# Loading a weight in place and early, moving a normalisation to ScalarE, and giving an early output its own banks

## The chip, the cores and the metric

The kernel runs on one core of a Trainium2 chip. The metric is the device time of one execution, in microseconds (us). The kernel before takes 285.63 us in the median of its first three runs (285.40 to 285.96). A program on one core has no second die to compare with, so its runs are called fast unless they lie more than 1.5% above the fastest of the same kernel.

## The reference, cut to what matters

The inputs are 2048 rows of 640 columns in bfloat16. The result is the sum of a residual, a state-space layer (A) and a gated MLP with a spatial product (B).

```python
xn = layernorm(x)
# A: a complex diagonal recurrence over the 2048 rows
Bu   = xn @ B_bar.T                       # B_bar = ((Lam_bar-1)/Lam) * B
h[t] = Lam_bar * h[t-1] + Bu[t]
yA   = 2 * real(h @ C.T) + xn * Dskip
# B: a gated MLP with a 2048 x 2048 product over the rows
z    = gelu(xn @ w_in)                    # 2048 x 1728
z1, z2 = z[:, :864], layernorm(z[:, 864:])
g    = w_sp @ z2 + b_sp[:, None]          # "spatial"
yB   = (z1 * g) @ w_out
out  = x + yA + yB
```

## The kernel before

The kernel records every operation with the memory that it reads and writes. A list scheduler with a cost model of its own then deals the operations to the engines' queues. In the timelines below an operation that is ready still waits for those that stand ahead of it in its engine's queue (the eviction "u2" of set 4 was ready near 162.4 us and ran at 166.1). And any edit can deal the queues anew.

TensorE runs these stages: z2 tiles, the "bu" products (41.8 to 86.8 us), z1 tiles (to 116), then eight "product sets" j = 0..7 of seven products each. A set multiplies one eighth of `w_sp` with z2 by a seven-product (Strassen-like) scheme and takes 10.2 us; S1 to S4 and T1 to T4 are the combinations (sums) of blocks of `w_sp` and of z2 that these products take, made by VectorE. After sets 5 and 6 come two "early outputs" each; the other twelve outputs end the kernel. One output is 20 products of states with C ("oh") and 14 products of gated rows with `w_out` ("og").

The parts that the change and the argument touch, with cuts marked `...`:

```python
# memory: r2 first holds the tables and scratch of the scan, later the transposed gate tiles gT.
# The raw C tiles are staged in the SAME bytes as gT:
q2 = r2.again()
wo_m = q2.sub(7 * 1280)
gT_m = [q2.sub(1792) for _ in range(8)]
cr_m = Mem(gT_m[0].lo, 8 * 1792)
craw_m = [cr_m.sub(1280) for _ in range(10)]
...
def c_scaled():                     # C' = kappa * C, complex; 10 tiles of 128 x 640
    for q in range(5):
        ...                         # DMA transposes: craw[2q] <- C_re, craw[2q+1] <- C_im
    for q in range(5):
        for c, (x, y, op) in ...:
            act(... activation(o, y, Identity, scale=k2) ...)          # "cy": ScalarE
            dve(... scalar_tensor_tensor(o, x, k1, o, mult, op) ...)   # "cp": VectorE
...
def spatial(j, banks):              # one product set, PSUM banks X, Y, Z
    prod(X, "A11", "B11"); ev(p1, X)          # ev: eviction of the bank by ScalarE
    prod(Y, "S1", "T1");   ev(p5, Y)
    prod(X, "S2", "T2");   ev(u2, X)          # the "third eviction"
    prod(Z, "A12", "B21"); dve(c11 = Z + p1)
    prod(X, "S3", "T3");   ev(u3, X) ...      # needs bank X free: waits for u2
    prod(Y, "S4", "B22");  dve(c12 = Y + u2)
    prod(X, "A22", "T4");  ev(c21, X)
    ...                                       # gate: 4 tiles in a ring, then gT by DMA transpose
...
for j in range(8):
    ...
    spatial(j, (0, 1, 2) if j % 2 == 0 else (3, 4, 5))
    ...
    if j >= 5 and j < 7:
        next_out(2, [6])                      # both early outputs in banks 6 and 7
next_out(12, [6, 0, 2, 4])
```

"fix" below means the 70 operations that add the scan's state to the states of each row block: ScalarE scales (P and Q), VectorE adds. "Horner" and "scan" are VectorE's recurrence over the rows.

## Time and profile before

| | before |
|---|---|
| time, median | 285.63 us |
| TensorE busy | 270.0 of 282.6 us |
| TensorE waits after start-up | 0.98 + 2.88 + 0.92 + 0.92 us |
| granted clock | 0.993: half speed for 3.41 us inside the run |

TensorE is busy nearly all the time and its order of work is the same in both kernels, so only its waits and its clock can change. These are two lines of the page of the kernel before: busy time by engine, and the granted TensorE clock in tenths of full speed, in 40 slices of the span.

```profile
...
PE 270.0 (96%) x1584; PEld 159.7 (57%) x1584; DVE 228.7 (81%) x556; ACT 158.4 (56%) x278; POOL 26.1 (9%) x53
...
PEclk9999999999999999999999979999999999999999
...
```

The view of waits, kernel before, TensorE alone from 100 to 225 us (engine, line waited for, releaser: us in total, times, longest us):

```profile
...
PE ps L923 <- ACT arena L936: 2.9, 1, 2.9
PE ps L1005 <- DVE arena L1022: 1.8, 2, 0.9
PE ps L923 <- ACT arena L602: 1.0, 1, 1.0
```

L923 is the product of a set and L936 its ScalarE eviction; L1005 is the first product of an output and L1022 VectorE's addition that empties its banks; L602 is the last z1 eviction. The largest wait is the 2.9 us inside set 4. The timeline of ScalarE in the kernel before, around that wait (start us, length us, engine, line, operation, count, and the idle time before it):

```profile
...
159.54 0.62 ACT L936 ACTIVATE arena<-ps,arena 128x432 f32<-128x432 f32 x1 [0.36 <-PE ps L923]
160.06 1.53 ACT L842 ACTIVATE arena<-arena 128x640 bf16<-128x640 bf16 x2
161.50 0.50 ACT L934 COPY arena<-ps 128x432 f32<-128x432 f32 x1
161.90 0.83 ACT L842 ACTIVATE arena<-arena 128x640 bf16<-128x640 bf16 x1
162.63 2.55 ACT L718 ACTIVATE arena<-arena 128x512 bf16<-128x512 bf16 x4
165.08 0.62 ACT L709 ACTIVATE arena<-arena 128x512 bf16<-128x512 bf16 x1
165.60 1.11 ACT L936 ACTIVATE arena<-ps,arena 128x432 bf16<-128x432 f32 x2
...
```

L842 are C scalings ("cy"), L718 and L709 fixes, L936 and L934 evictions. From 159.54 on ScalarE never rests. The last line holds c21 of set 3 and then u2 of set 4, the eviction on which the bank X depends. Its product had ended near 162.4, and it ran at 166.1. Ahead of it stood C scalings, four fix scalings, h7 and c21.

The second early output of each pair also waits. The timeline of TensorE, kernel before, has these lines for the state products of the first and the second output:

```profile
...
182.75 2.88 PE L1005 MATMUL ps<-arena 128*128 128x320 bf16 x20
...
188.45 2.89 PE L1005 MATMUL ps<-arena 128*128 128x320 bf16 x20 [0.92 <-DVE arena L1022]
...
```

The second could not start before VectorE had emptied banks 6 and 7 of the first. From start to start it is 5.70 us (188.45 less 182.75), of which 0.92 us is idle.

Lastly, busy time of each engine in three stretches, kernel before (stretch, its length, busy us with instruction counts, then PEclk, DMA share and GB/s):

```profile
...
core 0: us, PE busy (x) PEld busy (x) DVE busy (x) ACT busy (x) POOL busy (x), PEclk, DMA share, GB/s
40.00:60.00 20.00, 20.00 (x92) 8.73 (x91) 14.66 (x39) 18.53 (x37) 4.33 (x6) 1.00 0.55 72
60.00:80.00 20.00, 20.00 (x91) 8.52 (x89) 20.00 (x42) 11.84 (x20) 0.00 (x0) 1.00 0.00 1
...
167.00:171.00 4.00, 4.00 (x16) 1.85 (x15) 3.42 (x8) 2.74 (x6) 0.00 (x0) 0.68 0.79 94
...
```

In the last stretch the mean clock is 0.68. The trace's clock record says half speed for 3.41 us, from 166.17 to 169.58. TensorE resumed only at 166.77, so the first 0.6 us of the half speed fell into the wait. The same view, for the 3.41 us before the half speed and for the half speed itself:

```profile
...
162.76:166.17 3.41, 1.13 (x7) 0.39 (x4) 3.41 (x10) 3.41 (x7) 0.00 (x0) 1.00 1.16 270
166.17:169.58 3.41, 2.81 (x8) 1.20 (x9) 3.41 (x9) 2.38 (x5) 0.00 (x0) 0.50 1.06 136
...
```

TensorE was idle for 2.28 of the 3.41 us (3.41 less 1.13) just before its clock halved.

### The profile page before, as it was taken

Reading aid. Unit: us, or ns where it says so; the run is one execution under the profiler, and the core shown is the slowest. Engines: PE = TensorE matmul, PEld = TensorE weight load, DVE = VectorE, ACT = ScalarE, POOL = GpSimd, SP = SyncE. Lnnn points to the kernel's source line nnn. Section 1 sums busy time; section 2 is a strip of 40 time slices with the busy share of each in tenths; the row PEclk is TensorE's granted clock in tenths of the full one; section 3 lists DMA queues with packets and bytes.
Section 4 is the critical chain, followed back from the end, with each engine's and each line's share of the span. In section 5 each row is a group of like instructions: output and inputs, shape, how many; then the busy total and the mean of one; then the engine's idle time right before and its main releaser. Section 6 shows DMA issues by size and latency. Waiting matters only on the chain.

```text
span 282.6 us, 4366 instructions
## 1 busy us (share of the span) xinstructions
PE 270.0 (96%) x1584; PEld 159.7 (57%) x1584; DVE 228.7 (81%) x556; ACT 158.4 (56%) x278; POOL 26.1 (9%) x53
## 2 busy tenths in 40 slices
PE   7799999999999999899999959989989999999995
PEld 2455554444446777555555525555555577777773
DVE  4899845899999999899999998999999616354442
ACT  3799999985447554323323889999999300000000
POOL 4355732300000000000000000000000000000000
PEclk9999999999999999999999979999999999999999
DMA  7998999200000333696599898929965244422211
GB/s 205 277 223 141 224 131 153 26 3 0 0 0 32 127 125 125 205 143 130 119 153 180 147 200 200 239 63 183 195 167 118 80 58 110 126 74 67 72 46 46
DMA packets 81186, 34.73 MB, mean 123 GB/s; under 512 B 68526, under 2 KB 81166, under 8 KB 81166
## 3 DMA queue, kind: packets, MB, share of 16 engines
q1 hardware_dynamic: 81022, 34.39, 56.3%
q8 instruction: 12, 0.20, 0.3%
q10 hardware_dynamic: 144, 0.08, 0.1%
q14 instruction: 8, 0.07, 0.1%
HBM read 12.29 MB, written 6.18 MB: 65 GB/s over the span
## 4 chain that ended last, share of the span: by engine, by line
PE 91%; DVE 3%; ACT 3%; DMA 1%; POOL 1%; issue 0%; SPq 0%; DVEq 0%
PE ps L923 28%; PE ps L559 19%; PE ps L617 16%; PE ps L1005 16%; PE ps L1013 11%; DMA arena<-in_A_x_dram 1%; PE ps L532 1%; ACT arena L718 1%; ACT arena L842 1%; DVE arena L505 1%; DVE arena L518 1%; DVE arena L1022 1%; DVE arena L506 1%; POOL arena L513 0%; ACT arena L936 0%
## 5 line engine op out<-in xcount | busy, mean ns | idle before, releaser
L923 PE MATMUL ps<-arena 128*128 128x432 bf16 x448 | 83.8, 350 | 3.9 <-ACT arena L936 2.9
L923 PEld LDWEIGHTS ps<-arena 128*128 128x128 bf16 x448 | 44.1, 99 | 43.1 <-ACT arena L936 3.3
L559 PE MATMUL ps<-arena 128*128 128x432 bf16 x320 | 60.4, 346 | 0.0
L559 PEld LDWEIGHTS ps<-arena 128*128 128x128 bf16 x320 | 38.2, 121 | 18.0
L1005 PE MATMUL ps<-arena 128*128 128x320 bf16 x320 | 46.1, 299 | 1.8 <-DVE arena L1022 1.8
L617 PE MATMUL ps<-arena 128*128 128x512 bf16 x200 | 45.2, 386 | 0.0
L718 ACT ACTIVATE arena<-arena 128x512 bf16<-128x512 bf16 x70 | 44.4, 719 | 0.0
L1005 PEld LDWEIGHTS ps<-arena 128*128 128x128 bf16 x320 | 31.1, 98 | 14.9 <-DVE arena L1022 2.5
L936 ACT ACTIVATE arena<-ps,arena 128x432 f32<-128x432 f32 (+1 forms) x32 | 19.7, 618 | 29.0 <-PE ps L923 29.0
L617 PEld LDWEIGHTS ps<-arena 128*128 128x128 bf16 x200 | 19.2, 96 | 25.8
L1013 PE MATMUL ps<-arena 128*128 128x320 bf16 (+1 forms) x224 | 33.1, 299 | 0.0
L1022 DVE TENSOR_TENSOR arena<-ps,arena 128x640 bf16<-128x640 f32 x15 | 12.3, 822 | 22.3 <-PE ps L1013 22.3
L624 ACT CAST arena<-ps 128x512 bf16<-128x512 f32 x40 | 21.3, 593 | 13.2 <-PE ps L617 13.2
L721 DVE TENSOR_TENSOR arena<-arena 128x512 bf16<-128x512 bf16 x70 | 26.7, 415 | 1.0 <-ACT arena L718 1.0
L1013 PEld LDWEIGHTS ps<-arena 128*128 128x128 bf16 (+1 forms) x224 | 21.9, 98 | 8.5
L648 DVE SCALAR_TENSOR_TENSOR arena<-arena 128x512 f32<-128x512 bf16 x35 | 25.5, 745 | 0.0
L880 DVE TENSOR_TENSOR arena<-arena 128x1024 bf16<-128x1024 bf16 x32 | 21.6, 684 | 1.7 <-PE ps L923 1.7
L602 ACT ACTIVATE arena<-ps 128x864 bf16<-128x864 f32 x16 | 14.2, 890 | 13.5 <-PE ps L559 12.4
L670 DVE TENSOR_TENSOR arena<-arena 128x512 f32<-128x512 f32 (+2 forms) x40 | 21.4, 553 | 0.0
L653 DVE SCALAR_TENSOR_TENSOR arena<-arena 128x256 bf16<-128x256 bf16 (+1 forms) x35 | 16.6, 479 | 0.0
L650 DVE SCALAR_TENSOR_TENSOR arena<-arena 128x256 bf16<-128x256 bf16 (+1 forms) x35 | 16.5, 477 | 0.0
L573 ACT ACTIVATE arena<-arena 128x864 bf16<-128x864 bf16 x16 | 14.9, 937 | 0.0
(88 smaller groups left out, 220.2 us busy)
## 6 DMA issues: line engine op xcount, KB each, us to landing
arena<-in_A_x_dram SPq DMA_DIRECT2D x32, 160.0 KB, 2.8
z_scratch<-arena SPq DMA_DIRECT2D x16, 216.0 KB, 1.9
arena<-z_scratch SPq DMA_DIRECT2D x8, 432.0 KB, 3.9
out_dram<-arena SPq DMA_DIRECT2D x15, 160.0 KB, 1.8
arena<-in_B_w_in_dram SPq DMA_DIRECT2D x10, 216.0 KB, 3.3
arena<-in_B_w_out_dram SPq DMA_DIRECT2D x1, 960.0 KB, 5.8
arena<-in_B_w_sp_dram SPq DMA_TRANSPOSE x32, 4.2
arena<-arena SPq DMA_TRANSPOSE x20, 3.3
```

The costliest lines, as they stand in the source:

```text
L559: r = e.matmul(ps[:, b + h, 0:FG], lhs(k), winv[:, k, hcol * FH + h * FG:hcol * FH + (h + 1) * FG], start=(k == 0), stop=(k == ND - 1))
L617: r = e.matmul(ps[:, b + ri, :], btv[:, ri, k, q * 128:(q + 1) * 128], rhs[k], start=(k == 0), stop=(k == ND - 1))
L624: act(lambda e, ri=ri: e.copy(o[:, ri, :, half, :], ps[:, b + ri, :].rearrange("p (m j) -> p j m", j=4)), [bank(b + ri)], [l_iv(q, jg * 4 ...
L648: dve(lambda e: e.scalar_tensor_tensor(tv, prev, lr, cur, op0=ALU.mult, op1=ALU.add), pr + [l_iv(q, j)] + cr, [t.iv()], cd(512) + PTR, nm ...
L670: tt = lambda o, a, b, op: (lambda e: e.tensor_tensor(o, a, b, op))
L718: act(lambda e, pv=pv, hv=hv, lo=lo, sc=sc: e.activation(pv, hv[:, lo:lo + 2, 1:257], ACT.Identity, scale=sc), [h.iv(), Civ(cn)], [m.iv()] ...
L721: dve(lambda e, m=m, lq=lq: e.tensor_tensor(lq, lq, m.ap(512), ALU.add), li + [m.iv()], li, cd(512, 2), "fix%s%d%d" % (nm, q, j))
L880: dve(lambda e: e.tensor_tensor(o.ap(1024), x.ap(1024), y.ap(1024), op), [x.iv(), y.iv()], [o.iv()], cd(1024, 2), "%s_%d" % (name, j))
L923: r = e.matmul(ps[:, bk, 0:FG], lv_[:, k, :], rv[k], start=(first and k == 0), stop=(k == 7), skip_group_check=True)
L936: act(lambda e: e.activation(o, pb(bk), ACT.Identity, bias=bias), [bank(bk)] + bi, [dst], ca(FG, psum=True, ptr=1), name)
L1005: r = e.matmul(ps[:, b + n, 0:320], hv[:, o:o + 128], cpv[:, ri, q, n * 320:(n + 1) * 320], start=(q == 0 and ri == 0), stop=False, skip_g ...
L1013: r = e.matmul(ps[:, b + n, 0:320], gv[0:kk, k, :], wov[0:kk, k, n * 320:(n + 1) * 320], start=False, stop=(k == 6), skip_group_check=True)
```

## The change

The change has three parts. C is loaded directly to its final place as soon as the B weights there are dead (about 87 us), and is scaled in place with small temporaries in the dead z1 buffers. The normalisation of z2 row tiles 8 to 15 goes from VectorE to ScalarE. And the first of two early outputs uses banks that the next product set doesn't need yet, so that the second doesn't wait for its banks.

```diff
-        cr_m = Mem(gT_m[0].lo, 8 * 1792)
-        craw_m = [cr_m.sub(1280) for _ in range(10)]
+        cy_m = [Mem(z1o_m[0].lo, 3 * 1728).again()]
+        cy_m = [cy_m[0].sub(1280) for _ in range(4)]
...
+        ACT_Z2 = (8, 12)
...
+            if t0 in ACT_Z2:
+                dve(... v(7) = -mean * rstd ...)
             for i in range(t0, t1):
                 z = z2v[:, i, :]
+                if t0 in ACT_Z2:
+                    act(lambda e, i=i, z=z: e.activation(z, z, ACT.Identity, bias=st2v[:, 7, i:i + 1],
+                                                         scale=st2v[:, 6, i:i + 1]), ...)
+                    continue
                 dve(... (z - mean) * rstd ...)
...
-                    dma(... craw[2q], craw[2q+1] <- C_re, C_im ..., transpose=True)
+                    dma(... cpv[:, c, q, :] <- C_re, C_im ..., transpose=True)
...
-                    act(o = k2 * y);  dve(o = o +/- k1 * x)        # raw tiles to cpv
+                act(ta = k2 * im); act(tb = k2 * re)               # temporaries, two pairs
+                dve(re = k1 * re + ta); dve(im = tb - k1 * im)     # in place in cpv
...
-                next_out(2, [6])
+                next_out(2, [1 if j % 2 else 4, 6])
```

More of the change, by code (lines that the diff above doesn't have):

```diff
@@ L587, in z2_norm @@
                  0.33 + 0.165 * (t1 - t0), "z2r" + n)
+            if t0 in ACT_Z2:
+                dve(lambda e: e.scalar_tensor_tensor(v(7), v(2), -1.0, v(6), op0=ALU.mult, op1=ALU.mult),
+                    [vi(2), vi(6)], [vi(7)], 0.08, "z2b" + n)
             for i in range(t0, t1):
                 z = z2v[:, i, :]
+                if t0 in ACT_Z2:
+                    act(lambda e, i=i, z=z: e.activation(z, z, ACT.Identity, bias=st2v[:, 7, i:i + 1],
+                                                         scale=st2v[:, 6, i:i + 1]),
+                        [z2iv(i), s2iv(6, i, i + 1), s2iv(7, i, i + 1)], [z2iv(i)], ca(FH, ptr=2), "z2n%d" % i)
+                    continue
                 dve(lambda e, i=i, z=z: e.tensor_scalar(z, z, st2v[:, 2, i:i + 1], st2v[:, 6, i:i + 1],
@@ L831, in c_scaled @@
             for q in range(5):
-                raw = craw_m[2 * q:2 * q + 2]
-                for m, src, nm in ((raw[0], A_C_re, "r"), (raw[1], A_C_im, "i")):
-                    dma("sp", m.ap(D).rearrange("p (o n) -> p o n", o=1), src[:, q * 128:(q + 1) * 128], [], [m.iv()],
-                        D * 256, "C%s%d" % (nm, q), transpose=True)
+                for c, (src, nm) in enumerate(((A_C_re, "r"), (A_C_im, "i"))):
+                    dma("sp", cpv[:, c, q, :].rearrange("p (o n) -> p o n", o=1), src[:, q * 128:(q + 1) * 128], [],
+                        [cp_m.iv((c * 5 + q) * 1280, 1280)], D * 256, "C%s%d" % (nm, q), transpose=True)
@@ L836, in c_scaled @@
             for q in range(5):
-                re, im = craw_m[2 * q:2 * q + 2]
                 k1, k2 = C("k")[:, q:q + 1], C("k")[:, 5 + q:6 + q]
-                for c, (x, y, op) in enumerate(((re, im, ALU.add), (im, re, ALU.subtract))):
-                    o = cpv[:, c, q, :]
-                    oi = cp_m.iv((c * 5 + q) * 1280, 1280)
-                    act(lambda e, y=y, o=o, k2=k2: e.activation(o, y.ap(D), ACT.Identity, scale=k2),
-                        [y.iv(), Civ("k")], [oi], ca(D, ptr=1), "cy%d%d" % (q, c))
-                    dve(lambda e, o=o, x=x, k1=k1, op=op: e.scalar_tensor_tensor(
-                            o, x.ap(D), k1, o, op0=ALU.mult, op1=op, reverse1=(op == ALU.subtract)),
-                        [x.iv(), oi, Civ("k")], [oi], cd(D) + PTR, "cp%d%d" % (q, c))
+                re, im = cpv[:, 0, q, :], cpv[:, 1, q, :]
@@ new lines, in c_scaled @@
+                rei, imi = cp_m.iv(q * 1280, 1280), cp_m.iv((5 + q) * 1280, 1280)
+                ta, tb = cy_m[q % 2 * 2], cy_m[q % 2 * 2 + 1]
+                act(lambda e, o=ta, im=im, k2=k2: e.activation(o.ap(D), im, ACT.Identity, scale=k2),
+                    [imi, Civ("k")], [ta.iv()], ca(D, ptr=1), "cy%d0" % q)
+                act(lambda e, o=tb, re=re, k2=k2: e.activation(o.ap(D), re, ACT.Identity, scale=k2),
+                    [rei, Civ("k")], [tb.iv()], ca(D, ptr=1), "cy%d1" % q)
@@ L850, in t_comb @@
+                dve(lambda e, re=re, k1=k1, t=ta: e.scalar_tensor_tensor(re, re, k1, t.ap(D), op0=ALU.mult, op1=ALU.add),
+                    [rei, ta.iv(), Civ("k")], [rei], cd(D) + PTR, "cp%d0" % q)
+                dve(lambda e, im=im, k1=k1, t=tb: e.scalar_tensor_tensor(
+                        im, im, k1, t.ap(D), op0=ALU.mult, op1=ALU.subtract, reverse1=True),
+                    [imi, tb.iv(), Civ("k")], [imi], cd(D) + PTR, "cp%d1" % q)
         def t_comb(n):
```

## The prediction

> **What bounds it.** TensorE: busy 270.0 of 282.6 us (the page's first part), 91% of the chain of waits. Its order is the same in both kernels, so only its waits can go. The waits view shows: 0.98 us at 116.0 before the first product set, 2.88 us at 163.9 inside product set 4 (both on a ScalarE eviction), 0.93 + 0.86 us at 187.5 and 208.1, where the second early output waits for VectorE to empty the first's banks. The 2.88 us gap is followed by 8 matmuls 0.36 us apart instead of 0.18; the trace has the clock at half for 3.41 us from there, about 1.7 us lost. The Trainium skill ("TensorE: Matmul & The Clock Gate", Part 1) puts such a drop after an idle window of about 3.4 us; here 2.88 was enough and 0.9 to 1.0 us was not.
>
> **Cause of the big wait** (timeline). ScalarE runs without a pause from 159.5 to 167: seven C scalings (0.72 us apart), four "fix" scalings and h7 stand before the eviction that frees the bank. That one was ready at 162.4 and ran at 166.1. VectorE is full from 57 to 183, apart from about 1.4 us at 118.7, where the weight combination S4 of set 1 waits for a matmul to free its buffer.
>
> **What changes.**
> - C scaling: in the new order none of ScalarE's ten stands before that eviction, and VectorE's ten (0.80 us apart) stand among and after set 4's additions. Loads move to the z1 stage (DMA share 0.31 there), 1.25 us of queue time each: z1 stores may slip by 1 to 2 us, no TensorE wait expected.
> - z2 rows 8-15: VectorE loses 8 x 0.415 = 3.3 us, ScalarE gains 8 x about 1.0 (estimate: 0.72 for 512 columns, plus 352 x 0.83 ns), at 61-76 between evictions that take 0.96 of each 2.25 us: fits. I expect little from it: VectorE did that work while waiting for the sine tables (ready 54.5), and the T combinations that then filled the wait now come later. By a running sum of durations VectorE reaches S4 of set 1 near 117 to 119, waits there for the same matmul (120.1), and has 2.7 us of Horner/scan work behind that wait that stood ahead of it before.
> - Early outputs: both 0.9 us waits vanish, with 0.17 us of slower restart each: 2.1 us.
>
> **On the critical path.** Removed: 2.88 + 1.7 + 2.1 = 6.7 us. Returned: in the new order VectorE has, after set 4's fourth product at 163.7, about 15 us of work up to the last fix of row block 0, ending near 179; TensorE finishes set 5 at 178.3. The first early output should wait about 0.9 us, and slack at evictions of sets 4 and 5 is 0.2 to 0.4 us, so perhaps 0.4 more. Net about -5.4.
>
> **Time**: 280.2 us, 8 in 10 between 278.6 and 283.0. Faster by over 2%: 0.42, within 2%: 0.54, slower: 0.04.
>
> **To look for.** Right: no wait over 1.5 us inside sets 4-5; clock full from 20 us to the end; no wait at the second early outputs; a new wait of 0.5 to 2 us ahead of the first early output, on VectorE's fix or C addition; the wait at 116 unchanged; ScalarE near full at 60-80.
>
> **What would make it wrong.** A wait of 2 us or more inside set 4 or 5 again, halving the clock (283 and above); C transposes delaying z1 stores past three buffers; or VectorE gaining from the z2 move, so that the new wait vanishes (279).

The "running sum" in it works as follows: take each engine's new queue, give every operation the duration it has in the trace before, and carry the time forward, waiting where an operation needs another engine's result. The trace before gives 0.80 ns for each column (822 ns for 640 columns, 719 for 512, both with one per-partition operand), which leads to the same 1.0 us.

## The result, and the profile after

The changed kernel takes 279.17 us in the median (279.08 to 279.33, 4 runs), against 285.51 us (285.35 to 285.96, 4 runs) for the kernel before. The ratio is 0.9776, with a 95% interval from 0.9759 to 0.9793. Ratios here are the mean time of one kernel's fast runs over that of the other's fast runs of the same rounds, so they are not quite the ratio of the medians quoted.

The same lines of the page, kernel after:

```profile
...
PE 267.9 (97%) x1584; PEld 159.3 (57%) x1584; DVE 226.3 (82%) x550; ACT 166.7 (60%) x286; POOL 26.0 (9%) x53
...
PEclk9999999999999999999999999999999999999999
...
```

The clock is full from the second slice to the end, and TensorE's busy time is smaller by 2.1 us although it does the same matmuls (1.5 us of it in the product sets, where the half clock lay: 83.8 to 82.3 us). The waits of TensorE in the same window, kernel after:

```profile
...
PE ps L934 <- ACT arena L611: 1.0, 1, 1.0
PE ps L1016 <- DVE arena L730: 0.7, 1, 0.7
```

The wait in set 4 and both waits of the second early outputs are gone; the wait at the first set is unchanged. One wait is new: 0.7 us ahead of the first early output (L1016), on VectorE's last fix (L730). The timeline of ScalarE, kernel after, around u2 of set 4:

```profile
...
160.94 0.61 ACT L947 ACTIVATE arena<-ps,arena 128x432 bf16<-128x432 f32 x1
...
161.84 0.74 ACT L727 ACTIVATE arena<-arena 128x512 bf16<-128x512 bf16 x1
162.46 0.63 ACT L718 ACTIVATE arena<-arena 128x512 bf16<-128x512 bf16 x1
162.98 0.62 ACT L947 ACTIVATE arena<-ps,arena 128x432 f32<-128x432 f32 x1
164.12 0.83 ACT L849 ACTIVATE arena<-arena 128x640 bf16<-128x640 bf16 x1 [0.51 <-DVE arena L835]
...
```

Lines are numbered anew here: L947 and L945 are evictions, L727 fixes and L718 h7. The eviction u2 of set 4 is the line at 162.98. From 160.3 on only two fixes, c21 of set 3, the eviction p5 and h7 stand ahead of it; the first C scaling (L849) comes at 164.12. The timeline of TensorE, kernel after, at the first two outputs:

```profile
...
179.45 2.89 PE L1016 MATMUL ps<-arena 128*128 128x320 bf16 x20 [0.70 <-DVE arena L730]
...
184.08 2.88 PE L1016 MATMUL ps<-arena 128*128 128x320 bf16 x20
...
```

The second output (184.08) follows without an idle note, 4.63 us after the first: 1.07 us sooner than before. The three stretches, kernel after:

```profile
...
40.00:60.00 20.00, 20.00 (x93) 8.73 (x91) 11.29 (x35) 18.64 (x36) 4.14 (x6) 1.00 0.55 83
60.00:80.00 20.00, 20.00 (x91) 8.50 (x90) 17.95 (x37) 19.34 (x28) 0.00 (x0) 1.00 0.00 1
...
167.00:171.00 4.00, 4.00 (x24) 2.14 (x23) 4.00 (x7) 4.00 (x7) 0.00 (x0) 1.00 1.03 113
...
```

From 60 to 80 us ScalarE went from 11.84 to 19.34 us busy. VectorE is less busy by 5.4 us from 40 to 80 us: 3.3 us of that is the work moved away, and the rest is in the main waiting. The view of waits, kernel after, all engines, 40 to 225 us, has the T combinations (L870) waiting for ScalarE's normalised tiles (L595):

```profile
...
DVE arena L870 <- ACT arena L595: 2.0, 2, 1.7
...
```

### The profile page after: what moved, and what is told of

Read it like the earlier page. It is cut to its first block, busy times and chain, and to the rows that moved or that the text cites. A ratio compares the mean times of both kernels' runs of the same rounds, so it can differ in the third digit from the quotient of the medians.

```text
span 277.1 us, 4376 instructions
## 1 busy us (share of the span) xinstructions
PE 267.9 (97%) x1584; PEld 159.3 (57%) x1584; DVE 226.3 (82%) x550; ACT 166.7 (60%) x286; POOL 26.0 (9%) x53
## 4 chain that ended last, share of the span: by engine, by line
PE 88%; DVE 8%; DMA 1%; issue 1%; POOL 1%; ACT 0%; SPq 0%; DVEq 0%
PE ps L934 24%; PE ps L560 20%; PE ps L626 16%; PE ps L1016 16%; PE ps L1024 11%; DVE arena L854 1%; DVE arena L856 1%; DMA arena<-in_A_x_dram 1%; DVE arena L730 1%; PE ps L533 1%; DVE arena L506 1%; DVE arena L519 1%; DVE arena L891 1%; DVE arena L954 1%; DVE arena L507 1%
## 5 line engine op out<-in xcount | busy, mean ns | idle before, releaser
L934 PE MATMUL ps<-arena 128*128 128x432 bf16 x448 | 82.3, 346 | 1.0 <-ACT arena L611 1.0
L560 PE MATMUL ps<-arena 128*128 128x432 bf16 x320 | 60.4, 346 | 0.0
L1016 PE MATMUL ps<-arena 128*128 128x320 bf16 x320 | 46.1, 299 | 0.7 <-DVE arena L730 0.7
L727 ACT ACTIVATE arena<-arena 128x512 bf16<-128x512 bf16 x70 | 45.0, 713 | 1.0 <-DVE arena L730 0.9
L1016 PEld LDWEIGHTS ps<-arena 128*128 128x128 bf16 x320 | 31.2, 98 | 13.5 <-DVE arena L730 1.1
L947 ACT ACTIVATE arena<-ps,arena 128x432 f32<-128x432 f32 (+1 forms) x32 | 19.8, 617 | 29.1 <-PE ps L934 29.0
L730 DVE TENSOR_TENSOR arena<-arena 128x512 bf16<-128x512 bf16 x70 | 26.4, 418 | 1.3 <-ACT arena L727 1.1
L611 ACT ACTIVATE arena<-ps 128x864 bf16<-128x864 f32 x16 | 14.2, 890 | 13.5 <-PE ps L560 12.5
L679 DVE TENSOR_TENSOR arena<-arena 128x512 f32<-128x512 f32 (+2 forms) x40 | 21.2, 547 | 0.0
```

Source lines behind the costliest of these rows:

```text
L560: r = e.matmul(ps[:, b + h, 0:FG], lhs(k), winv[:, k, hcol * FH + h * FG:hcol * FH + (h + 1) * FG], start=(k == 0), stop=(k == ND - 1))
L679: tt = lambda o, a, b, op: (lambda e: e.tensor_tensor(o, a, b, op))
L727: act(lambda e, pv=pv, hv=hv, lo=lo, sc=sc: e.activation(pv, hv[:, lo:lo + 2, 1:257], ACT.Identity, scale=sc), [h.iv(), Civ(cn)], [m.iv()] ...
L730: dve(lambda e, m=m, lq=lq: e.tensor_tensor(lq, lq, m.ap(512), ALU.add), li + [m.iv()], li, cd(512, 2), "fix%s%d%d" % (nm, q, j))
L934: r = e.matmul(ps[:, bk, 0:FG], lv_[:, k, :], rv[k], start=(first and k == 0), stop=(k == 7), skip_group_check=True)
L947: act(lambda e: e.activation(o, pb(bk), ACT.Identity, bias=bias), [bank(bk)] + bi, [dst], ca(FG, psum=True, ptr=1), name)
```

## The experiments

All kernels gave correct results.

### The C part alone

Edit: the kernel after with `ACT_Z2 = ()` and `next_out(2, [6])`.

> The C part alone on the kernel before (early load, in-place scaling; no z2 move, no new banks). Theory (the 2.88 us wait in product set 4 came from where the C scaling stood, and its clock drop hangs on that wait): no wait over 0.5 us inside sets 4 and 5, clock full after start-up, the two waits of the second early outputs stay at about 1 us each; -2.9 -1.7 = -4.6 us, about 280.9 us. Rival (VectorE is simply overfull, and only less work on it helps): set 4 still waits about 2 to 3 us, over 284 us.

Measured: 280.72 us in the median (280.38 to 282.09, 4 runs), ratio 0.9856 (0.9795 to 0.9917). Waits of TensorE, 100 to 225 us:

```profile
...
PE ps L1016 <- DVE arena L1033: 1.9, 2, 1.0
PE ps L934 <- ACT arena L611: 1.0, 1, 1.0
```

The wait in set 4 is gone, and only the two output waits and the wait at the first set (L611) are left. That last one is the same in all the kernels here but two, and is left out of most answers below. The rival, that an overfull VectorE must first lose work, falls: VectorE has the same 556 instructions here as before and is as busy (229.2 us against 228.7). Nor do scalings ahead of u2 make the wait by themselves: in this trace two still run right before it (162.12 and 162.85; u2 at 163.57), but c21 of set 3 and the fixes came earlier. One of the four runs (282.09 us) has a clock of 0.994; its trace is not kept.

### What of the C part did it: the same memory dependence put back

Edit on the C part alone: the data stay in their final place, and each load and each VectorE scaling is also made to touch the old staging tile.

```diff
+        cr_m = Mem(gT_m[0].lo, 8 * 1792)
+        craw_m = [cr_m.sub(1280) for _ in range(10)]
-                        [cp_m.iv((c * 5 + q) * 1280, 1280)], D * 256, ...
+                        [cp_m.iv((c * 5 + q) * 1280, 1280), craw_m[2 * q + c].iv()], D * 256, ...
-                    [rei, ta.iv(), Civ("k")], [rei], ...          # and the same for im
+                    [rei, ta.iv(), Civ("k"), craw_m[2 * q].iv(), craw_m[2 * q + 1].iv()], [rei], ...
```

> As c_only, C is loaded into and scaled in its final place, but each load and scaling is also made to depend on the old staging tile's memory, which it no longer uses: so it waits for the scan's scratch as before, and the transposed gate tiles wait for it as before. Theory (the shared memory set the order of the queues): the wait in set 4 is back, 3 to 3.5 us on the third ScalarE eviction, clock halved after it; 285 to 286.5 us, the same as before. Rival (in-place scaling itself, or the different operation mix, is the gain): about 281 us.

Measured: 285.62 us in the median (285.45 to 286.63, 4 runs), ratio 1.0026 (0.9966 to 1.0086): the same as the kernel before.

```profile
...
PE ps L936 <- ACT arena L949: 3.2, 1, 3.2
PE ps L1018 <- DVE arena L1035: 1.8, 2, 0.9
...
```

Nothing but bookkeeping differs from the fast version, and the 3 us wait is back. So the gain of the C part comes from breaking a dependence on memory, not from scaling in place.

That dependence has two halves. C cannot be loaded before the scan has left its scratch, and the transposed gate tiles cannot be written before C is scaled. Three looks (one run each) put back one half or both on the C part alone.

```diff
 # gate tiles wait for the scaling ("early, gate tiles wait"):
-                    [rei, ta.iv(), Civ("k")], [rei], ...
+                    [rei, ta.iv(), Civ("k"), ("al", 2560 * q, 2560 * q + 2560)], [rei], ...
-            dma("sp", t.ap(896)..., gm.ap(896), [gm.iv()], [t.iv()], ...)
+            dma("sp", t.ap(896)..., gm.ap(896), [gm.iv()], [t.iv(), ("al", n % 8 * 1792, n % 8 * 1792 + 1792)], ...)
 # loads wait for the last scan ("late, gate tiles free"):
-            dve(... "sd%d" ..., [Bm.iv()], ...)
+            dve(... "sd%d" ..., [Bm.iv()] + ([("tok", 0, 1)] if q == 4 else []), ...)
-                    dma("sp", cpv[:, c, q, :]..., [], ...)
+                    dma("sp", cpv[:, c, q, :]..., [("tok", 0, 1)], ...)
```

Early, gate tiles wait:

> c_only with one half of the old memory dependence put back: the transposed gate tiles wait for the scaling of the C tiles whose memory they used to share, while the loads stay early. Theory (both halves together are needed to delay the chain): no wait over 0.5 us in set 4, 281 us. Rival (the wait of the gate tiles for the scaling alone is the cause): a wait of about 3 us in set 4, about 285.5 us.

Measured: 281.39 us.

```profile
...
PE ps L1017 <- DVE arena L1034: 2.5, 2, 1.5
...
```

Late, gate tiles free:

> c_only with the other half put back: C loads wait until the last scan has read its scratch (about 150 us), gate tiles do not wait for the scaling. Theory: no wait over 0.5 us in set 4, perhaps 0.5 to 1 us more around the first outputs than c_only, 281 to 282.5 us. Rival (early loading alone is the gain): a wait of about 3 us in set 4, about 285.5 us.

Measured: 282.20 us.

```profile
...
PE ps L1016 <- DVE arena L1033: 2.9, 2, 1.9
...
PE ps L934 <- ACT arena L947: 0.5, 1, 0.5
```

Both:

> Both halves put back on c_only: late loads and gate tiles that wait for the scaling. Theory: the wait in set 4 is back at about 3.3 us with the clock halved after it, and some new wait around the first outputs: 286 to 288 us. Rival (neither dependence matters): about 281 us.

Measured: 289.06 us, 1 us over the top of what was expected.

```profile
...
PE ps L934 <- ACT arena L947: 3.1, 1, 3.1
PE ps L1017 <- DVE arena L1034: 2.9, 2, 2.0
...
PE ps L1017 <- DVE arena L856: 0.2, 1, 0.2
```

The wait of about 3 us in set 4 appears only with both halves. Either half alone costs little, 0.7 and 1.5 us over the median of the C part (one run each), at the outputs. The extra microsecond of the last has a likely source in its clock record: the clock halves twice, for 3.41 us after the wait in set 4, and again for 3.41 us after a 2.0 us wait at an output, which the expectation had left out.

How the dependence reaches TensorE can be followed in the queues: late C, late scaling, late gT transposes, gate tiles held in their ring of four, the gating of set 2 late in VectorE's queue, c21 of set 3 behind it on ScalarE, and u2 of set 4 behind c21. That the two halves are needed is shown; this chain between them and the wait is read from the queues and was not cut link by link. In the trace before, ScalarE was not idle ahead of u2: the delay had become an order of the queue, which the scheduler had dealt from that chain in its own model.

### The z2 part alone, and the change without it

Edit of the first: the kernel before with the z2 lines of the diff. Edit of the second: the kernel after with

```diff
-        ACT_Z2 = (8, 12)
+        ACT_Z2 = ()
```

> The z2 part alone on the kernel before. Theory (VectorE did the z2 work in a pause, and the new order puts 2.7 us of Horner and scan work behind its wait for a matmul at 120 us): no gain, the wait in set 4 grows from 2.9 to about 5 us; 287 to 288.5 us. Rival (the change's plain intent: VectorE is full from 57 to 183 us and loses 3.3 us of work): 282 to 284 us.

Measured: 287.54 us in the median (287.33 to 289.30, 4 runs), ratio 1.0100 (1.0035 to 1.0164): slower by 1%, which is clear of 1. All four runs have a lowered clock (0.982 to 0.988).

```profile
...
PE ps L932 <- ACT arena L945: 4.7, 1, 4.7
PE ps L1014 <- DVE arena L1031: 1.8, 2, 0.9
...
```

> The changed kernel with the z2 move undone. Theory: the 0.7 us wait ahead of the first early output vanishes and nothing comes instead: 278.2 to 278.6 us, 0.6 to 1.0 us below the changed kernel. Rival (the z2 move is part of the gain): 281 to 282 us.

Measured: 277.94 us in the median (277.85 to 278.40, 4 runs), ratio 0.9748 (0.9682 to 0.9815). Waits of TensorE:

```profile
...
PE ps L934 <- ACT arena L611: 1.0, 1, 1.0
```

Moving 3.3 us of work off a VectorE that is full from 57 to 183 us makes the kernel slower, alone and within the change. The reason, as read from the queues, is where that work stood. Below are the lines of VectorE's scan (L679 or L688: shortest/median/longest ns, first and last start) in the kernel before, after, z2 part alone, and the change without it, in this order.

```profile
...
L679 DVE TENSOR_TENSOR_SCAN arena<-arena x10: 661/680/692, 84.8 to 147.5; 128x256 f32<-128x256 f32 x10
...
```

```profile
...
L688 DVE TENSOR_TENSOR_SCAN arena<-arena x10: 654/676/684, 88.4 to 154.1; 128x256 f32<-128x256 f32 x10
...
```

```profile
...
L688 DVE TENSOR_TENSOR_SCAN arena<-arena x10: 662/682/686, 88.4 to 150.4; 128x256 f32<-128x256 f32 x10
...
```

```profile
...
L688 DVE TENSOR_TENSOR_SCAN arena<-arena x10: 662/683/701, 85.3 to 151.3; 128x256 f32<-128x256 f32 x10
...
```

With the z2 move the first scan starts at 88.4 instead of about 85, and the last scan 2.9 us later than in the kernel before (z2 part alone), or 2.8 us later than without the move (kernel after against the change without it). The removed work had filled a pause in which VectorE waited for the sine tables: with the move VectorE idles 2.25 us until 54.8, where the kernel before does normalisation and T combinations. The T combinations then had to wait for ScalarE, and the new order put Horner work behind a fixed wait for a matmul at 120 us. The loss is shown by both runs, and its size and the grown wait in set 4 (4.7 us) were expected; these links were not cut one by one. A late last scan is no loss by itself: without the z2 move it starts at 151.3, later than before, in the faster kernel.

### The banks alone, and the change without them

Edit of the first: `next_out(2, [1 if j % 2 else 4, 6])` in the kernel before. Edit of the second: `next_out(2, [6])` in the kernel after.

> Only the early outputs' banks changed on the kernel before. Theory: both waits of the second early outputs (0.93 and 0.86 us, each with about 0.17 us of slower restart) vanish, the wait in set 4 and the half clock stay: -2.1 us, about 283.4 us. Rival (VectorE, full at that time, only moves the wait elsewhere): 285 us or more.

Measured: 283.43 us in the median (281.57 to 283.48, 4 runs), ratio 0.9935 (0.9882 to 0.9989).

```profile
...
PE ps L923 <- ACT arena L936: 2.9, 1, 2.9
...
```

> The changed kernel with the early outputs' banks as before. Theory: both waits of the second early outputs come back, 0.9 to 1.25 us each, since VectorE is no less full than before: 281.2 to 281.8 us, about 2.1 to 2.6 us above the changed kernel. Rival (the emptier VectorE drains the first output in time): below 280 us.

Measured: 281.51 us in the median (281.38 to 283.67, 4 runs), ratio 0.9917 (0.9870 to 0.9963).

```profile
...
PE ps L1016 <- DVE arena L1033: 2.1, 2, 1.1
...
PE ps L1016 <- DVE arena L730: 0.7, 1, 0.7
```

This part is worth 1.7 us on the kernel before (285.15 us, the median in the same rounds, to 283.43; the expectation said 2.1) and 2.3 us within the change (281.51 against 279.17). Runs with and without a half clock are mixed in these medians; the three half-clock runs of the first, 283.39 to 283.48, lie 1.9 us under the four of the kernel before in the same rounds (means), and the three full-clock runs of the second, 281.38 to 281.53, 2.3 us over the kernel after. And the wait of set 4 stays at 2.9 us in the first, and the new wait of 0.7 us stays in the second. So the output waits, the one in set 4 and the new one come and go separately in these runs.

### The new wait at the first output

Edit on the kernel after: the first output runs its gate products before its state products.

```diff
+            gfirst = (j, half) == (0, 0)
...
-            pe(mmh, ...)
-            pe(mmg, ...)
+            for f in ((pe_g, pe_h) if gfirst else (pe_h, pe_g)):
+                f()
```

(The start and stop flags of the accumulation follow the order.)

> The changed kernel, z2 move kept, but the very first output runs its 14 gate products before its 20 state products, which need every fix and C tile. Theory (the new 0.7 us wait is on VectorE's last fix, and TensorE has 1.9 us of other work for that output): the wait goes, 278.2 to 278.5 us. Rival (VectorE falls behind by as much elsewhere): 279 us or more.

Measured: 278.32 us in the median (278.01 to 278.59, 4 runs), ratio 0.9783 (0.9738 to 0.9828); 0.85 us below the kernel after.

```profile
...
PE ps L934 <- ACT arena L611: 1.0, 1, 1.0
```

The wait is gone. So it was for VectorE's fixes, which only the state products need, and 1.9 us of other work for TensorE covers it. The two medians are of different jobs, but all eight runs have a clock of 0.998 or more, and the two sets don't overlap.

### The last wait, and a version that beats both

Edit: exchange the bank triples of the product sets, so that set 0 doesn't need the bank of the last z1 eviction.

```diff
-            spatial(j, (0, 1, 2) if j % 2 == 0 else (3, 4, 5))
+            spatial(j, (3, 4, 5) if j % 2 == 0 else (0, 1, 2))
...
-                next_out(2, [1 if j % 2 else 4, 6])
+                next_out(2, [4 if j % 2 else 1, 6])
```

On the kernel after:

> The exchange of the bank triples alone on the changed kernel, z2 move kept. A running sum over its new order says that the wait at 116 us goes, but that VectorE's last fix comes about 3.3 us after the first early output could start: 280.5 to 281.5 us, or 1.2 to 1.7 us more if the clock halves after that wait. Rival (a wait removed is a gain kept): 278.2 us.

Measured: 282.09 us, clock 0.994.

```profile
...
PE ps L1016 <- DVE arena L730: 3.1, 1, 3.1
```

The 1.0 us wait is gone and a 3.1 us wait has come, with a half clock of 3.41 us after it. A wait taken away was not a gain kept. The running sum over the new queues had forecast this wait (3.3 us on the last fix): the edit dealt VectorE's queue anew. Without the z2 move the same exchange works:

> The changed kernel with the z2 move undone and the two bank triples of the product sets exchanged (set 0 in banks 3 to 5), so that the first product no longer waits for the last z1 eviction, which holds banks 0 and 1; the early outputs' banks exchanged with them. Theory: the 0.98 us wait at 116 us goes and no other comes: about 277.0 us, 0.9 to 1.0 us below the run without the z2 move. Rival (the new order of the queues, dealt anew by any edit, brings a wait elsewhere): 278 us or more.

Measured: 277.17 us in the median (276.83 to 277.44, 6 runs), ratio 0.9746 (0.9716 to 0.9777). TensorE has no wait left between 100 and 225 us in its profile. This is the best version found, 2.0 us below the changed kernel by the medians (of different jobs).

## Why the prediction was right

- **Time.** 280.2 us was predicted, within 278.6 and 283.0; 279.17 was measured. The chance was put at 0.42 for faster by over 2%, and 0.54 for within 2%; it fell just on the faster side. The span, which the argument was about, fell by 5.5 us (282.6 to 277.1), where 5.4 was expected. The other 0.9 us of the 6.3 us between the medians is not explained by the two profiles; part of it is that the profiled execution of the kernel before, 284.99 us, was 0.5 us faster than its median. Start to start, the traces give 3.05 us for the wait in set 4, 1.4 for the half clock and 2.1 for the outputs, less 0.87 for the new wait and 0.26 because the first set starts later (117.25 against 116.99): 5.4. So the forecast of 5.4 is that close partly by luck, as its misses cancel: the clock 0.3 too large, 0.4 for thin slack that did not come, and the later start not foreseen. That the time fell on the side of "faster by over 2%" is luck too, as the third point shows.
- **The wait in set 4 and its clock.** Right: both vanished in the profile of the C part alone, which gave 4.7 us by the medians where 4.6 was expected. (Four of the seven runs of the kernel before in those rounds had a lowered clock. Full-clock runs alone, 284.04 to 280.60 us in the mean, differ by 3.4 us; the wait alone costs 3.05 from start to start.) The prediction named the place in ScalarE's queue. It did not see why the queue was so; the experiments showed two halves of a memory dependence, both needed.
- **The clock term is a chance from run to run.** The prediction took 1.7 us as certain; the trace before shows 1.4. In the 25 runs of the kernel before in the three jobs, 11 had a clock of 0.999 or more and took 283.19 to 284.34 us; the other 14 had 0.994 or less and took 284.91 to 287.60 (the last of these counts as slow). So a lowered clock is there in somewhat over half of the executions. In the eight kernels whose profile has no wait of 2.0 us or more after start-up, 2 of 28 executions have one. So most of it comes with the wait in set 4. The rounds behind the headline ratio saw only the latter times. Against the 11 full-clock runs alone the change is worth 4.7 us (mean 283.85 to 279.17, of different jobs), or 1.6%.
- **What decides the chance.** The kept traces show more than the prediction saw. In all 14 the clock changes only at multiples of 3.413 us, counted from the first entry of the clock record. Take these steps as windows and add up TensorE's idle time in each. Of the windows at full speed after that entry, every one with 2.01 us idle or more is followed by half speed, and none with 1.94 us or less. Around set 4 the idle time in the window is 2.28 us (kernel before), 2.26 (banks alone), 2.89 (z2 part alone), 3.14 (memory dependence put back) and 3.10 (both halves). The closest pair is two waits at the outputs, of "late, gate tiles free" and "both" (window, its length, TensorE busy):

```profile
...
183.96:187.37 3.41, 1.47 (x12) 1.02 (x12) 3.41 (x8) 3.41 (x7) 0.00 (x0) 1.00 1.00 178
...
188.29:191.71 3.42, 1.41 (x11) 0.81 (x10) 3.42 (x9) 3.42 (x6) 0.00 (x0) 1.00 1.16 254
...
```

  After the first the clock stays full; after the second it halves for 3.41 us. So a wait of 2.88 us halves the clock when enough of it falls into one window, and need not when a window's edge cuts it near the middle. This can be why 11 of 25 executions escaped; no trace of one of them is kept, so that is not shown.
- **Early outputs.** Right: 2.1 us expected, 1.7 measured alone by the medians (1.9 by half-clock runs alone) and 2.3 within the change. The trace has 0.92 us for both waits; the prediction's 0.86 is not in it. What the text called "slower restart" is not slower work: the products take as long with and without a wait (2.89 and 2.88 us in the two timelines). Each wait costs 1.07 us from start to start, not 0.92, since the overlap of one product group with the next (0.16 us in the timeline after: 182.17 and 2.07 less 184.08) is lost as well.
- **z2.** Right, and stronger than put: "I expect little from it" was a loss of 1.2 us within the change (medians of different jobs), and of 2.1 us alone. ScalarE's new operations took 1.12 us each in the median; the estimate of about 1.0 was their distance when they follow each other. The VectorE wait at S4 of set 1 came as said: it ended at 120.39 us.
- **The new wait.** Right in place (VectorE's last fix before the first early output) and near in size: 0.7 us, where 0.9 was expected. The further 0.4 us for thin slack did not come: u2 of set 4 ended about 0.4 us before its bank was needed (163.60 against 163.99), and no wait showed in sets 4 and 5. The z1 stores did not hold up either: ScalarE's one wait for them is 1.0 us, against 1.1 before.
- **The skill pages.** "TensorE: Matmul & The Clock Gate", Part 1, puts the drop after at least one idle window of about 3.4 us, in a window that runs freely. A 2.88 us gap, 2.28 us of it in one window, was enough in this trace. For ScalarE, "ScalarE: Activation LUTs", section "What ACT_TABLE_LOAD costs", gives 186 ns plus 0.833 ns for each column plus about 93 ns for each per-partition operand. For 864 columns and two such operands that is an estimate of 1.09 us; the trace has a median of 1.118 us, so it agrees within 3%.

## What to carry to other kernels

When an engine's queue is in order, ask of each wait which operations stand ahead of the one waited for, and which shared memory put them there: a buffer reused for two purposes can order the queues far away from both. Work taken off a busy engine is worth nothing if it stood in a pause, and less than nothing if it moves other work behind a fixed wait; carry the new queues forward with measured durations before trusting an average load. Test each part of a change alone, since here one of three parts was a loss hidden under two gains.

## What the Trainium skill lacked or had wrong

- "TensorE: Matmul & The Clock Gate" (Part 1, and the table under "Why this matters for your kernels": "No PE-idle gaps >~3µs between matmul bursts"): gaps under 3 us can halve the clock too. A gap of 2.88 us goes with a half clock in the profile before, and 14 of 25 executions of that kernel showed a lowered clock. A wait of 2.0 us was followed by a half clock in one look, and one of 1.9 us was not in another.
- The same page, where the table says "One MID window of idle": a window need not be idle throughout, and the page gives no figure for how much is enough. In these 14 profiles 2.01 us of 3.41 was enough (up to 3.14 inside the runs), and 1.94 was not. One of these windows lay in start-up: 2.09 us idle, then half speed from 8.15 to 11.56 us (the change without the banks). So a lowered clock in a run without a trace doesn't tell which wait made it.
- The same page's window of 3413 ns, which it calls free-running, is no error: half-clock stretches inside the runs were 3.41 us or, after a 4.7 us wait, 6.83 us; the full-clock stretches of the profile before, 160.43 and 112.64 us, are 47 and 33 times 3.413 us; and the clock record's first entry lies anywhere from 3.97 to 7.28 us after the start of the span.
